# Weight sums and low parts on VectorE, and the keys' second copy by DMA, in an attention kernel with two dense layers

## The chip, the cores and the metric

The kernel runs on one core of one Trainium2 chip. The metric is the time of one execution on the device in microseconds. Three runs of the kernel before took 1054.61, 1055.4 and 1058.65 us; the median is 1055.4 us.

## The reference

Causal attention with a decay per position (4 batches, 8 heads, 576 positions, head size 64), then two dense blocks on 2304 tokens of width 512, each with an inner width of 2048. All in fp32:

```python
scores = q @ k.T / 8 + (cum[:, None] - cum[None, :])     # cum = cumsum(log(clip(f)))
scores = where(causal, -1e9, scores)
x = softmax(scores) @ v                  # heads side by side: 2304 x 512
x = relu(x @ w_in1) ** 2 @ w_out1        # first layer
out = elu(x @ w_in2) @ w_out2            # second layer
```

## The kernel before

Every product is made of three: a number is split into a high part, rounded to the type that TensorE takes (a copy by ScalarE, `AF.Copy`), and a low part, the number minus its high part; then high times high, high times low and low times high are added up (`mm3`, `three`). The low parts are the work of `less` (L131, GpSimd) and `minus` (L115, VectorE or, by `less`, GpSimd). Tables of letters say which engine does which step: a is ScalarE, v VectorE, p GpSimd and, for the keys' copy, d a DMA.

The time falls into these stages:

- **Attention, to about 366 us.** Heads are loaded, scored and applied one after the other. Batch 0 takes plain fp32 operands (`Plain`); batches 1 to 3 take split ones, made by `load_head` (L293) with `part == "F"`, the third letter of each table. Per head: ScalarE copies the raw rows of queries and keys to `qk1` (L312); SP's queue fetches four extra rows into `qk2` (L319); GpSimd subtracts the queries' high part (L320); `kh` copies the keys' high part from `qk1` to `qk2` (L321 to L324, by VectorE); GpSimd subtracts the keys' high part (L325) and splits the values. Scores then take two products, one from `qk1` (L337), one from `qk2` (L338). While heads run, `unit` does half of the first layer for 256 tokens at a time, as filler for TensorE.
- **First layer, the rest, to about 652 us.** `first_layer(j, nxt)` takes blocks j of 512 tokens in the order 3, 4, 0, 1, 2 (block 4 has 256). Blocks 0 to 2 do the inner chunks 8 to 15 here; each chunk has a product `pH`, a `relu2` (relu by ScalarE, square `g` and low part `gl` by VectorE, high part `gh` by ScalarE) and a product into `O`, two chunks later. At a block's end `operands` forms the seven sums that the second layer reads (subtractions on GpSimd, L822; low parts `yl` by GpSimd and VectorE in turn) and stores them by SP's queue (L819).
- **Second layer, from about 652 us.** The inner width is cut into eight pairs of 128-wide chunks, four in the first half, four in the second. `first_product` makes a step's four quarter products from seven products of 128x256 (take and add: `hs`), then elu, `gh` and `gl`; `second_product` follows one step later.

The weights of the second layer come as 64-bit words. `next_w` takes a raw tile, asks SP's queue for the next (`ask_w`, two buffers), and `words` puts the fp32 number together: one ScalarE and four VectorE instructions of 128x512 (L150 to L154). `pair_weights(p)` makes one pair in three steps, each up to a `yield`: first two word tiles, seven high parts of 128x256 by ScalarE (L911), seven low parts (L912) and four sums (L915); then twice one word tile with one high part (L933) and one low part (L934) of 128x512. The chain `wl2` of these steps is advanced at fixed places: three steps beside block 0, four beside block 1 (L1074), five in block 2 (L1077), the rest at the second layer's steps 4 to 6 and 18 to 21 (`w_at`).

Which instruction comes when on each engine is set ahead of the run by a planner (L1150, `schedule_with_timeline_sim=True`): it orders each engine's instructions by their place in the program and by its own cost of each; at run time an engine takes them in that order, and so does SP's queue for DMAs.

Of the kernel before, what the change touches and what calls it, by code (L numbers as in the profile page):

```python
# [43 lines left out]

PLAIN_B = 4
CP = {'pA': 'a', 'pB': 'av', 'xA': 'a', 'xB': 'a'}
ENG = {'qk': 'aaa', 'ql': 'ppp', 'kh': 'pvv', 'kl': 'ppp', 'vh': 'ppp', 'vl': 'ppp', 'xl': 'pv'}
NORM = 'ap'
GL = 'pv'
SQ = 'appp'  # L50
# [19 lines left out]
def f32(ap):  # L70
    return ap.bitcast(F32)
# [10 lines left out]
def attention_then_moe_kernel(ctx, tc, first, firstv, plain, qkv, aug0, f, w1, w2, out):  # L82
    nc = tc.nc
# [31 lines left out]
    def minus(eng, dst, x, hi):  # L115
        if eng == "p":
            less(dst, x, hi)
        else:
            nc.vector.tensor_tensor(dst, x, f32(hi), op=ALU.subtract)  # L119

    def copy(eng, dst, x, scale=None):
        if eng == "a":
            nc.scalar.activation(out=dst, in_=x, func=AF.Copy, scale=1.0 if scale is None else scale)  # L123
        elif eng == "p":
            nc.gpsimd.tensor_scalar(dst, x, 1.0 if scale is None else scale, 0.0, op0=ALU.mult, op1=ALU.add)
        elif scale is None:
            nc.vector.tensor_copy(dst, x)
        else:
            nc.vector.tensor_scalar(dst, x, scale, None, op0=ALU.mult)

    def less(dst, x, hi):  # L131
        nc.gpsimd.tensor_tensor(out=dst, in0=x, in1=f32(hi), op=ALU.subtract)  # L132
# [40 lines left out]
    def win(m, fc, part_, c):  # L173
        return wslot[m, fc][:, part_, c * 128:(c + 1) * 128]

    def wout(m, fc, part_, c=None):
        o = wslot[m, fc][:, part_, 512:1024]
        return o if c is None else o[:, c * 128:(c + 1) * 128]

    def mm3(dst, pairs, first, last, skip=False):  # L180
        n = len(pairs)
        for i, (l, r) in enumerate(pairs):
            nc.tensor.matmul(out=dst, lhsT=l, rhs=r, start=first and i == 0,  # L183
                             stop=last and i == n - 1, skip_group_check=skip)

    def three(hl, hr):
        return [(hl[0], hr[0]), (hl[1], hr[0]), (hl[0], hr[1])]
# [105 lines left out]
    def load_head(b, h, part):  # L293
# [12 lines left out]
        if part == "A":  # L306
            ac = slice(Q0, QW + 256)
            copy(ENG["qk"][w], qk1[:, ac], raw[:, ac])
        else:
            ac = slice(0, RAW)  # L310
            if part == "F":
                copy(ENG["qk"][w], qk1, raw[:, ac])  # L312
            else:
                copy(ENG["qk"][w], qk1[:, qc], raw[:, qc])
                copy(ENG["qk"][w], qk1[:, kc], raw[:, kc])
        if part == "A":
            nc.sync.dma_start(out=f32(qk2[64:68, ac]), in_=f32(ca[g:g + 1]))
        else:
            nc.sync.dma_start(out=f32(qk2[64:68, ac]), in_=aug[g, :, ac])  # L319
        minus(ENG["ql"][w], qk2[0:64, qc], raw[0:64, qc], qk1[0:64, qc])  # L320
        if ENG["kh"][w] == "d":  # L321
            nc.sync.dma_start(out=f32(qk2[0:64, kc]), in_=f32(qk1[0:64, kc]))
# [242 lines left out]
    def relu2(h, n, eng, sq):  # L565
        g = mg.tile([128, 512], F32, tag="g", name="g", bufs=2)
        gh = mg.tile([128, 512], F32R, tag="gh", name="gh")
        gl = mg.tile([128, 512], F32R, tag="gl", name="gl")
        nc.scalar.activation(out=g[:, 0:n], in_=h[:, 0:n], func=AF.Relu)  # L569
        if sq == "a":  # L570
            nc.scalar.activation(out=g[:, 0:n], in_=g[:, 0:n], func=AF.Square)
        else:
            (nc.vector if sq == "v" else nc.gpsimd).tensor_tensor(out=g[:, 0:n], in0=g[:, 0:n], in1=g[:, 0:n], op=ALU.mult)  # L573
        nc.scalar.activation(out=gh[:, 0:n], in_=g[:, 0:n], func=AF.Copy)  # L574
        minus(eng, gl[:, 0:n], g[:, 0:n], gh[:, 0:n])
        return gh, gl
# [63 lines left out]
    def interleave(main, n_main, side, n_side):  # L640
        done = 0
        for i, _ in enumerate(main):
            while done * n_main < (i + 1) * n_side:
                if next(side, "end") == "end":
                    break
                done += 1
        return done

    def chain(gens):
        for g in gens:  # L650
            yield from g
# [129 lines left out]
    def fetch1(j):  # L781
        t0, n = blocks[j]
        xq[j] = []
        for c in range(NC):
            x = x_tile([128, 2, n])
            for off, step, b, s in runs(t0, n):
                nc.sync.dma_start(out=f32(x[:, :, off:off + step]), in_=x1[b][c::NC, :, s:s + step].rearrange("c p t -> p c t"))
            xq[j].append(x)
# [11 lines left out]
    def h_tile():  # L800
        n_ph[0] += 1
        return (ps_H3 if n_ph[0] % 4 else ps_H1).tile([128, 512], F32, tag="H", name="pH")
# [41 lines left out]
    def first_layer(j, nxt):  # L844
        t0, n = blocks[j]
        whole = t0 >= NU * CH
        x = xq.pop(j)
        if nxt is not None:
            fetch1(nxt)
        pr = xa.tile([128, NC, 512], F32, tag="xu", name="pr")  # L850
        if not whole:
            for i in range(n // CH):
                nc.sync.dma_start(out=pr[:, :, i * CH:(i + 1) * CH], in_=part[t0 // CH + i])
        po = [ps_O.tile([128, 512], F32, tag=f"O{c}", name=f"O{c}") for c in range(NC)]
        f0 = 0 if whole else 8

        def second_b(fc, gh, gl):
            for c in range(NC):
                mm3(po[c][:, 0:n], three([wout(1, fc, t, c) for t in range(2)], [gh[:, 0:n], gl[:, 0:n]]), fc == f0, fc == 15)

        pend, depth = [], DEPTH1 * 512 // n
        for fc in range(f0, 16):
            ph = h_tile()
            for c in range(NC):
                mm3(ph[:, 0:n], three([win(1, fc, t, c) for t in range(2)], [x[c][:, 0], x[c][:, 1]]), c == 0, c == NC - 1)
            g = relu2(ph, n, GL[1], "v")
            pend.append((fc, *g))
            if len(pend) > depth:
                second_b(*pend.pop(0))
            yield  # L870
        for p in pend:
            second_b(*p)
        for c in range(NC):
            y = pr[:, c, 0:n]
            if whole:
                nc.vector.tensor_copy(y, po[c][:, 0:n])
            else:
                nc.vector.tensor_tensor(y, po[c][:, 0:n], y, op=ALU.add)
        operands(j, pr)
        yield  # L880
# [13 lines left out]
    def next_w():  # L894
        t = words(ahead.pop(0))
        ask_w()
        return f32(t)

    def w_tile(shape):
        k = n_w[0] % 16  # L900
        n_w[0] += 1
        return (wa, wb)[k // 8].tile(shape, F32R, tag=f"w{k}", name=f"v{k}")

    def pair_weights(p):
        wi = [w_tile([128, 4, 2, 256]), w_tile([128, 3, 2, 256])]
        wo = w_tile([128, 2, 2, 512])
        wp[p] = wi, wo

        def op(a, k):
            h, l = (wi[k // 4][:, k % 4, r] for r in range(2))  # L910
            nc.scalar.activation(out=h, in_=a, func=AF.Copy)  # L911
            less(l, a, h)  # L912

        def add(out, x, y, f):
            nc.gpsimd.tensor_tensor(out=out, in0=x, in1=y, op=f)  # L915

        ta, tb = (next_w() for i in range(2))
        a11, a12, a21, a22 = (t[:, c:c + 256] for t in (ta, tb) for c in (0, 256))
        op(a11, 0)
        op(a12, 5)  # L920
        op(a22, 4)
        add(a22, a21, a22, ALU.add)
        add(a21, a11, a21, ALU.subtract)
        add(a11, a22, a11, ALU.subtract)
        add(a12, a12, a11, ALU.subtract)
        op(a22, 3)
        op(a21, 2)
        op(a11, 1)
        op(a12, 6)
        yield  # L930
        for i in range(2):
            t = next_w()
            nc.scalar.activation(out=wo[:, i, 0], in_=t, func=AF.Copy)  # L933
            less(wo[:, i, 1], t, wo[:, i, 0])  # L934
            yield

    def fetch2(j, ks):
        for k in ks:
            if k >= x2[j].shape[0]:
                continue  # L940
            x = x_tile([128, 2, 2, 256])
            nc.sync.dma_start(out=f32(x).rearrange("p r c t -> p r (c t)"), in_=x2[j][k])
            xq.setdefault(j, []).append(x)
# [126 lines left out]
    ask_w()  # L1070
    ask_w()
    wl2 = chain(pair_weights(p) for p in range(8))
    interleave(first_layer(0, 1), 9, wl2, 3)
    interleave(first_layer(1, 2), 9, wl2, 4)  # L1074
    fetch2(4, range(0, 2))
    for i, _ in enumerate(first_layer(2, None)):
        if i in (3, 4, 5, 6, 7):  # L1077
            next(wl2)
    fetch2(4, range(2, 3))
    fetch2(3, range(0, 6))  # L1080
# [7 lines left out]
    for s, (half, j, p) in enumerate(steps):  # L1088
        q = p % 4
        if q == 0:  # L1090
            x = xq.pop(j)
# [62 lines left out]
```

## Time and profile before

| | |
|---|---|
| median of 3 runs | 1055.4 us |
| profiled execution | 1054.71 us |
| its span, first to last instruction | 1052.7 us |
| busy: TensorE, its weight loads | 1010.2 us (96%), 889.1 us (84%) |
| busy: VectorE, ScalarE, GpSimd | 691.1 us (66%), 545.8 us (52%), 375.4 us (36%) |
| mean granted TensorE clock | 0.997 of full speed |

One execution was taken by the hardware profiler. Times count from the span's start. An engine is busy while one of its instructions runs; for matmuls, which are pipelined, the ends are modelled, so a busy TensorE is not one at its peak. PE is TensorE, PEld its weight loads, DVE VectorE, ACT ScalarE, POOL GpSimd, SP the queue that issues most DMAs. A line is `L` and its number in the kernel; where a helper records the operation (L132 for `less`, L119 for `minus` on VectorE), the tiles tell which step it is: `v` is a tile of the second layer's weights, `wt` a word tile.

### The profile page before, as it was taken

What the parts mean: (1) busy time and instruction counts of PE and PEld (TensorE: products, weight loads), DVE (VectorE), ACT (ScalarE), POOL (GpSimd) and SP (SyncE); (2) the same over time, 40 slices, a digit from 0 to 9 for tenths busy, and PEclk for the clock granted to TensorE, in tenths of its full rate; (3) what the DMA queues carried; (4) which work ended last, traced back from release to release, by engine and by line L of the source; (5) the groups of instructions that cost most, each with busy time, mean ns of one, the idle gap of its engine ahead of it and who ended that gap; (6) DMA issues with size and microseconds to landing.
All of it is one profiled execution on the core that took longest, in us unless ns stands there. A gap on an engine that the chain in (4) does not pass through costs nothing.

```text
span 1052.7 us, 17378 instructions
## 1 busy us (share of the span) xinstructions
PE 1010.2 (96%) x6272; PEld 889.1 (84%) x6272; DVE 691.1 (66%) x1462; ACT 545.8 (52%) x1218; POOL 375.4 (36%) x400
## 2 busy tenths in 40 slices
PE   5899999999999999999999997999999999999998
PEld 3577788999999988889988775898988888899987
DVE  5993587776776548845467858695555878655554
ACT  4865688877886634424343434454334555333331
POOL 3556587576774300012144565440000445000000
PEclk9999999999999999999999999999999999999999
DMA  8843444543431074442645545625315365444502
GB/s 248 240 145 134 153 138 142 181 137 128 160 120 45 33 253 138 122 138 103 201 142 204 193 158 178 225 85 196 132 48 180 124 217 166 134 151 122 169 21 80
DMA packets 71960, 154.91 MB, mean 147 GB/s; under 512 B 8932, under 2 KB 34276, under 8 KB 71844
## 3 DMA queue, kind: packets, MB, share of 16 engines
q1 hardware_dynamic: 71812, 153.75, 44.8%
q8 instruction: 49, 0.80, 0.3%
q14 instruction: 35, 0.29, 0.1%
q10 hardware_dynamic: 64, 0.07, 0.0%
HBM read 115.15 MB, written 39.22 MB: 147 GB/s over the span
## 4 chain that ended last, share of the span: by engine, by line
PE 59%; issue 16%; DVE 12%; POOL 5%; ACT 4%; DMA 3%; SPq 0%; POOLq 0%; ACTq 0%; DVEq 0%
PE O L183 18%; PE pH L183 9%; PE P L183 8%; PE o L183 6%; PE ph L183 6%; PE pt L405 4%; PE pv L412 3%; DVE wt L153 2%; POOL v L132 2%; PE s L337 2%; PE s L338 2%; DVE wt L151 1%; POOL wt L915 1%; DVE wt L152 1%; PE pv L409 1%
## 5 line engine op out<-in xcount | busy, mean ns | idle before, releaser
L183 PEld LDWEIGHTS P<-xu,v 128*128 128x128 f32 x1536 | 200.3, 189 | 12.9 <-ACT hs L995 2.7
L183 PE MATMUL P<-xu,v 128*128 128x256 f32 x1536 | 203.5, 283 | 3.2 <-ACT hs L995 2.5
L183 PE MATMUL O<-v,gh 128*128 128x512 f32 x576 | 172.5, 395 | 0.6 <-ACT gh L966 0.5
L132 POOL TENSOR_TENSOR v<-wt,v 128x256 fp32r<-128x256 f32 (+1 forms) x72 | 72.5, 1015 | 211.7 <-ACT v L911 155.9
L183 PE MATMUL pH<-xu,w 128*128 128x512 f32 (+1 forms) x672 | 140.7, 360 | 0.0
L183 PEld LDWEIGHTS pH<-xu,w 128*128 128x128 f32 x672 | 114.0, 188 | 20.1
L183 PE MATMUL O<-gh,w 128*128 128x512 f32 (+1 forms) x448 | 122.8, 363 | 5.1 <-ACT gh L574 5.1
L183 PEld LDWEIGHTS O<-v,gh 128*128 128x128 f32 x576 | 103.4, 189 | 19.0 <-ACT gh L966 0.7
L995 ACT ACTIVATE hs<-P 128x256 f32<-128x256 f32 x128 | 47.9, 380 | 114.1 <-PE P L183 113.7
L183 PE MATMUL O<-v,gl 128*128 128x512 f32 x288 | 104.2, 394 | 0.5 <-DVE gl L988 0.5
L183 PEld LDWEIGHTS O<-gh,w 128*128 128x128 f32 x448 | 79.7, 189 | 19.9 <-ACT gh L574 6.2
L132 POOL TENSOR_TENSOR qk<-raw,qk 64x704 fp32r<-64x704 f32 (+1 forms) x48 | 78.9, 1643 | 20.4 <-ACT qk L123 15.2
L183 PE MATMUL O<-gl,w 128*128 128x512 f32 (+1 forms) x224 | 80.4, 365 | 3.9 <-DVE gl L119 3.9
L998 DVE TENSOR_TENSOR hs<-P,hs 128x256 f32<-128x256 f32 x96 | 40.4, 421 | 64.3 <-PE P L183 62.6
L132 POOL TENSOR_TENSOR yl<-pr,yh 128x512 fp32r<-128x512 f32 x18 | 24.7, 1371 | 158.7 <-ACT yh L815 108.2
L183 PE MATMUL o<-gh,w 128*128 128x256 f32 x384 | 76.6, 292 | 1.2 <-DVE xB L437 1.2
L150 ACT ACTIVATE wt<-wraw 128x512 f32<-128x512 f32 x57 | 38.2, 671 | 61.6 <-DMA wraw<-in_w_dram 38.6
L574 ACT ACTIVATE gh<-g 128x512 fp32r<-128x512 f32 (+1 forms) x80 | 46.8, 585 | 43.0 <-DVE g L573 39.1
L183 PE MATMUL ph<-xu,w 128*128 128x256 f32 x480 | 67.2, 287 | 1.3 <-DMA xu<-x 1.0
L1024 DVE TENSOR_TENSOR gl<-g,gh 128x512 fp32r<-128x512 f32 x64 | 47.3, 738 | 28.4 <-ACT gh L966 27.9
L573 DVE TENSOR_TENSOR g<-g 128x512 f32<-128x512 f32 (+1 forms) x56 | 45.4, 810 | 28.3 <-ACT g L569 28.2
L183 PEld LDWEIGHTS O<-v,gl 128*128 128x128 f32 x288 | 53.3, 188 | 11.6 <-DVE gl L988 0.8
(151 smaller groups left out, 2122.7 us busy)
## 6 DMA issues: line engine op xcount, KB each, us to landing
xu<-x SPq DMA_DIRECT2D x66, 512.0 KB
wraw<-in_w_dram SPq DMA_DIRECT2D x57, 512.0 KB
raw<-in_qkv_dram SPq DMA_DIRECT2D x24, 800.0 KB
x<-yh SPq DMA_DIRECT2D x31, 256.0 KB
x<-yl SPq DMA_DIRECT2D x31, 256.0 KB
x<-xs SPq DMA_DIRECT2D x16, 320.0 KB
xu<-x SPq DMA_DIRECT2D x16, 256.0 KB
raws_w<-in_w_dram SPq DMA_DIRECT2D x7, 512.0 KB
```

What stands on the lines that cost most here:

```text
L132: nc.gpsimd.tensor_tensor(out=dst, in0=x, in1=f32(hi), op=ALU.subtract)
L150: nc.scalar.activation(out=f32(t), in_=f32(hi), func=AF.Abs)
L153: nc.vector.scalar_tensor_tensor(t, hi, -0x40000000, t, op0=ALU.bitwise_and, op1=ALU.bitwise_or)
L183: nc.tensor.matmul(out=dst, lhsT=l, rhs=r, start=first and i == 0, stop=last and i == n - 1, skip_group_check=skip)
L337: nc.tensor.matmul(out=dst, lhsT=qk1[:, q0:q0 + 128], rhs=qk1[:, QW + j0:QW + j0 + n], start=first, stop=False)
L405: seen[0] = nc.tensor.transpose(dst, src, ident[:, c0:c0 + 128])
L412: seen[0] = nc.tensor.matmul(out=dst, lhsT=hh[2][:, J, :], rhs=hl[i], start=first and i == 0, stop=last and i == 1)
L573: (nc.vector if sq == "v" else nc.gpsimd).tensor_tensor(out=g[:, 0:n], in0=g[:, 0:n], in1=g[:, 0:n], op=ALU.mult)
L574: nc.scalar.activation(out=gh[:, 0:n], in_=g[:, 0:n], func=AF.Copy)
L995: nc.scalar.activation(out=o, in_=x, func=AF.Copy)
L998: nc.vector.tensor_tensor(o, y, x, op=ALU.add)
L1024: nc.vector.tensor_tensor(hl[i][1], gs[i], f32(hl[i][0]), op=ALU.subtract)
```

## The change

It has three parts. The low parts and the sums of `pair_weights` go from GpSimd to VectorE; the subtractions of `operands` (L822) and half of its low parts stay on GpSimd. The third pair's first step moves from the seventh chunk of block 1 to behind the first chunk of block 2; as there are three steps beside block 1 now, pair 1's are spread over the whole block. For the split heads, `kh` becomes a DMA on SP's queue from `qk1` to `qk2`, by a branch that the kernel had (L322).

```diff
-ENG = {'qk': 'aaa', 'ql': 'ppp', 'kh': 'pvv', 'kl': 'ppp', 'vh': 'ppp', 'vl': 'ppp', 'xl': 'pv'}
+ENG = {'qk': 'aaa', 'ql': 'ppp', 'kh': 'pvd', 'kl': 'ppp', 'vh': 'ppp', 'vl': 'ppp', 'xl': 'pv'}
...
         def op(a, k):
             h, l = (wi[k // 4][:, k % 4, r] for r in range(2))
             nc.scalar.activation(out=h, in_=a, func=AF.Copy)
-            less(l, a, h)
+            minus('v', l, a, h)
 
         def add(out, x, y, f):
-            nc.gpsimd.tensor_tensor(out=out, in0=x, in1=y, op=f)
+            nc.vector.tensor_tensor(out, x, y, op=f)
...
             nc.scalar.activation(out=wo[:, i, 0], in_=t, func=AF.Copy)
-            less(wo[:, i, 1], t, wo[:, i, 0])
+            minus('v', wo[:, i, 1], t, wo[:, i, 0])
...
-    interleave(first_layer(1, 2), 9, wl2, 4)
+    interleave(first_layer(1, 2), 9, wl2, 3)
     fetch2(4, range(0, 2))
     for i, _ in enumerate(first_layer(2, None)):
-        if i in (3, 4, 5, 6, 7):
+        if i in (0, 3, 4, 5, 6, 7):
             next(wl2)
```

## Rows read from the trace of the kernel before

**Rows 1.** Busy time by stretch: PE, PEld, DVE, ACT, POOL, granted clock, DMA share, GB/s.
```profile
600.00:675.00 75.00, 65.45 (x320) 53.00 (x319) 54.58 (x75) 32.93 (x63) 46.15 (x42) 1.00 0.57 204
725.00:800.00 75.00, 75.00 (x470) 67.57 (x469) 39.16 (x75) 29.46 (x62) 0.00 (x0) 1.00 0.31 106
815.00:885.00 70.00, 66.22 (x397) 58.43 (x396) 58.98 (x102) 38.76 (x85) 32.83 (x35) 0.98 0.48 160
```

**Rows 2.** The same view, attention with split heads.
```profile
86.00:225.00 139.00, 135.03 (x971) 119.24 (x970) 91.93 (x286) 105.47 (x262) 96.96 (x105) 1.00 0.43 140
```

**Rows 3.** Waits of PE, 600 to 680 us: total, times, longest.
```profile
PE O L183 <- ACT gh L574: 5.1, 3, 2.4
PE O L183 <- DVE gl L119: 3.9, 5, 1.6
```

**Rows 4.** Timeline at 600 us: start, duration, engine, line; idle before in brackets.
```profile
599.53 0.66 ACT L150 ACTIVATE wt<-wraw 128x512 f32<-128x512 f32 x1 [2.73 <-DMA wraw<-in_w_dram]
...
602.12 0.50 PE L183 MATMUL O<-gh,w 128*128 128x512 f32 x1 [1.36 <-ACT gh L574]
```

**Rows 5.** Timeline at 638 us.
```profile
638.05 1.28 POOL L132 TENSOR_TENSOR v<-wt,v 128x512 fp32r<-128x512 f32 x1 [2.24 <-ACT v L933]
638.05 1.56 DVE L152 TENSOR_SCALAR wt<-wt 128x512 int32<-128x512 int32 x1
```

**Rows 6.** Groups of DVE, 725 to 800 us: busy us, mean ns | idle before.
```profile
L1024 DVE TENSOR_TENSOR gl<-g,gh 128x512 fp32r<-128x512 f32 x14 | 9.7, 692 | 7.0 <-ACT gh L966 6.8
...
L1017 DVE TENSOR_SCALAR g<-hs 128x512 f32<-128x512 f32 x7 | 3.0, 427 | 0.2
L1016 DVE TENSOR_TENSOR hs<-hs 128x256 f32<-128x256 f32 x7 | 3.0, 425 | 3.1 <-ACT hs L995 3.0
```

**Rows 7.** Timeline at 648 us.
```profile
647.67 0.42 ACT L911 ACTIVATE v<-wt 128x256 fp32r<-128x256 f32 x1 [1.49 <-POOL wt L915]
```

**Rows 8.** Instructions with a word tile, by stretch: DVE, ACT, POOL busy (count).
```profile
600.00:675.00 75.00, 21.54 (x28) 12.13 (x25) 23.29 (x26) 1.00 0.57 204
815.00:885.00 70.00, 24.84 (x40) 17.27 (x35) 32.83 (x35) 0.98 0.48 160
```

**Rows 9.** Groups of DVE, 600 to 675 us.
```profile
L119 DVE TENSOR_TENSOR gl<-g,gh 128x512 fp32r<-128x512 f32 x9 | 8.6, 953 | 5.4 <-ACT gh L574 5.4
...
L153 DVE SCALAR_TENSOR_TENSOR wt<-wraw,wt 128x512 int32<-128x512 int32 x7 | 6.8, 968 | 0.2
L152 DVE TENSOR_SCALAR wt<-wt 128x512 int32<-128x512 int32 x7 | 6.6, 940 | 0.2
L119 DVE TENSOR_TENSOR yl<-pr,yh 128x512 fp32r<-128x512 f32 x6 | 6.5, 1089 | 4.0 <-DMA x<-yl 2.2 <-ACT yh L815 1.2 <-POOL v L132 0.6
```

**Rows 10.** Groups of DVE, 815 to 885 us.
```profile
L1024 DVE TENSOR_TENSOR gl<-g,gh 128x512 fp32r<-128x512 f32 x12 | 10.0, 831 | 4.7 <-ACT gh L966 4.5
...
L1016 DVE TENSOR_TENSOR hs<-hs 128x256 f32<-128x256 f32 x6 | 4.0, 668 | 0.0
L1017 DVE TENSOR_SCALAR g<-hs 128x512 f32<-128x512 f32 x6 | 4.0, 663 | 0.1
```

**Rows 11.** The tile `qk`: ns min/median/max; below, who waited for it (us, times).
```profile
L127 DVE CAST qk<-qk x24: 442/480/1923, 87.4 to 318.1; 64x576 fp32r<-64x576 f32 x24
...
  DVE qk L127: 12.1, 13
```

**Rows 12.** Timeline of one head at 300 us: cast, two subtractions, first score.
```profile
300.70 0.45 DVE L127 CAST qk<-qk 64x576 fp32r<-64x576 f32 x1 [1.10 <-ACT qk L123]
...
301.45 3.24 POOL L132 TENSOR_TENSOR qk<-raw,qk 64x704 fp32r<-64x704 f32 x2
...
305.83 0.36 PE L337 MATMUL s<-qk 128*128 128x256 f32 x1
```

**Rows 13.** The chain that ended last, a landing at 132 us.
```profile
131.89 4.87 DMA xu<-x
```

**Rows 14.** Waits of SP's queue: total, times, longest.
```profile
SPq L448 <- DVE xs L119: 60.6, 13, 10.4
```

## The prediction

> **What bounds the kernel now.** I read the busy time by stretch first. TensorE is the busiest engine and mostly has no gap: in 725 to 800 us it is busy for 75.00 of 75 us [rows 1]. What can be won is the time in which it waits. After the start-up there are three places with such time: 86 to 225 us (attention, 139 − 135.03 = 4.0 us idle [rows 2]), 600 to 675 us (end of the first layer, 75 − 65.45 = 9.55 us) and 815 to 885 us (70 − 66.22 = 3.8 us; the granted clock there is 0.98 in the mean, so some 0.04 of the stretch ran at 1.2 instead of 2.4 GHz, which cost about 1.4 us more) [rows 1]. Together that is 18.7 us, 1.8% of the span. Then I read the waits: who ended TensorE's. In 600 to 680 us they are ScalarE's `gh` and VectorE's `gl` [rows 3]. GpSimd, from which the change takes work, ends none of the two. So it counts only by what it holds up on the other two.
>
> In order of time around these waits, the trace shows three ways. At 599.5 us ScalarE, which takes its instructions in order, sat idle for 2.73 us before the third pair's second word group, because its raw weights had not landed; the relu behind it came late and TensorE waited 1.36 us for `gh` [rows 4]. At 638.05 us a GpSimd subtraction of 1.28 us and a VectorE shift start together, and the shift takes 1.56 us where a one-input instruction of that size takes 0.427 us without GpSimd [rows 5, 6]. At 647.7 us ScalarE sat 1.49 us until a GpSimd sum was done, with the next `gh` queued behind [rows 7].
>
> **The change, part by part.**
>
> *Lows and sums go to VectorE, stretch 600 to 675 us.* GpSimd does 26 of these instructions there in 23.29 us [rows 8]: 4 of 128x512 (two for each of two pairs), the other 22 of 128x256. On VectorE, a two-input 128x256 subtraction or sum takes 0.425 us (L1016) and a 128x512 one 0.692 us (L1024) [rows 6]. So VectorE gains 22 × 0.425 + 4 × 0.692 = 12.1 us of work. It loses a part of what it now spends beside GpSimd: `gl` 9 × (0.953 − 0.692) = 2.3 us, L152 7 × (0.940 − 0.427) = 3.6 us, `yl` 6 × (1.089 − 0.692) = 2.4 us, L153 7 × (0.968 − 0.692) = 1.9 us, 10.2 us in all [rows 6, 9]. Of GpSimd's 46.15 us there [rows 1], 23.29 go away; the subtractions of L822 and the `yl` stay. So about half, 5.1 us, is relief (bounds: none and 10.2). VectorE goes from 54.58 to 61.6 of 75 us: fuller, not full. Of TensorE's 9.55 us I count these as gone: the wait at 602 us and its echo, 1.9 us, since the third pair's words now come after the layer's end; some 2 us of waits behind ScalarE's stops for GpSimd sums; half of the other 5.6 us, which follow stretched VectorE instructions. Against that, 12.1 us of new work ahead of some squares and `gl` may delay TensorE; I put 1.7 us. Result: −5 us (bounds −9.5, when all waits go, and +3.5, when half of the net new 7.0 us of VectorE work lands on TensorE).
>
> The Trainium skill, SBUF — State Buffer, section Who interferes with whom, says that a VectorE instruction with two SBUF inputs contends with a GpSimd instruction that reads SBUF, and that the one that issues second waits until the first is done. The trace agrees (1.56 us against 0.427 [rows 5, 6]). It speaks against the change: the moved instructions have two SBUF inputs themselves, so they would stand still behind L822 and the `yl` as others do now. If this ate the relief, VectorE would have 66.7 of 75 us here and I would put this part at 0, the sum at 1055 us: the first rival below.
>
> *The third pair's step is later.* Its two word groups, seven copies, seven lows, four sums and two fetches of raw weights on SP's queue move from the last chunks of block 1 to behind the first chunk of block 2, past block 1's fourteen operand stores and the two operand fetches of L1075. Pair 1's steps spread over the same block. Between the new place and the first product that reads the third pair lie seven chunks of block 2 and the products of the first two pairs, most of the 75 us; so I cost the delay at nothing. If that cover were gone, TensorE would wait for weights, which it does nowhere now: its waits there are for `gh` and `gl` [rows 3]. The gain of 1.9 us above is this edit's.
>
> *Lows and sums in 815 to 885 us.* Here pairs 5 to 7 are made beside the second layer, and GpSimd does nothing else: 35 instructions, 32.83 us [rows 1, 8], 4 large (pairs 5 and 6) and 31 small. On VectorE: 31 × 0.425 + 4 × 0.692 = 15.9 us. Relief: `gl` 12 × (0.831 − 0.692) = 1.7, L1016 6 × (0.668 − 0.425) = 1.5, L1017 6 × (0.663 − 0.427) = 1.4, together 4.6 us [rows 6, 10]; the 40 word instructions took 24.84 us [rows 8] where 20 × 0.692 + 20 × 0.427 would be 22.4, another 2.4 us. So +15.9 − 7.0 = +8.9 us, and VectorE goes from 58.98 to 67.9 of 70 us, 97%. This is the weak place. For it: the chain of a pair's seven copies and four sums gets shorter, as a step of some 0.9 us on GpSimd (32.83 us for 35) becomes 0.425, and the lock that stretched instructions is gone entirely. Against it: no room is left. Bounds: −5.2 us (all of the 3.8 + 1.4 goes) and +9 us (all net work lands on TensorE). I take +1, nearer the middle.
>
> *The keys' second copy by DMA.* VectorE loses 24 casts (median 0.480 us, the longest 1.923) and the 12.1 us in 13 places in which it stood for ScalarE's copy [rows 11]. New on SP: 24 DMAs of 64 × 576 × 4 bytes = 147 KB, each of which stands until ScalarE's copy is done, up to 1.27 us, with the stores of x1, the fetches of x1 and of later heads queued behind. Cover: the head at 299 us has its cast at 300.70 us, GpSimd's two subtractions of the same head end at 304.69 and its first score is at 305.83 [rows 12]. A landing has taken up to 4.87 us in the chain [rows 13], so from 0 to 5.1 us after the cast's start, that is still no wait. No row shows this DMA itself, so its landing is bounded by that. TensorE's idle time in attention is 4.0 us [rows 2]; VectorE has 92 of 139 us busy there, and its waits are only some of the causes. I take −1 us (bounds −4 and +4, the latter by the third rival). After 225 us TensorE has no gap to speak of until 600 us, so what is won early stays won.
>
> Sum: −5 + 1 − 1 = −5 us. The profiled execution took 1054.71 us (span 1052.7, 2.0 us around it), 0.7 us under the median of 1055.4. 1054.7 − 5 = 1049.7, so **1050 us**. A planner fixes each engine's order ahead of the run and will choose other orders from 86 us on; no row tells which, and I allow 2 us either way for it.
>
> **Rivals.**
> 1. *No change*: the waits of 600 to 675 us move from `gh` behind GpSimd to `gl` behind longer VectorE queues, and the early gain is lost in 815 to 885 us. For it: `gl` already ends 3.9 us of waits [rows 3]. GpSimd keeps 46.15 − 23.29 = 22.9 us in 600 to 675 us, behind which the moved instructions can stand still as L152 does now. Against: ScalarE's stops [rows 4, 7] have causes that go. Time: 1054 to 1055 us.
> 2. *VectorE becomes the bound* (slower). Place: 815 to 885 us, then 600 to 675. Each low now stands in VectorE's queue for ScalarE's copy of its quarter, with `hs`, `g` and `gl` of the running products behind it. If the lows wait there, or GpSimd's lock stays, it pays +9 us in the later stretch and +3.5 in the earlier, with nothing won but the 1 us in attention: 1054.7 + 11.5 = 1066 us; where only half of it comes true, 1060. It decides from the point where VectorE can't hold 90% busy in 815 to 885 us: 67.9 / 0.9 = 75 us of work time in a 70 us stretch. For it: VectorE is already busy 58.98 of 70 us. Against: 11 us of idle time there are mostly ScalarE and GpSimd steps that get shorter.
> 3. *SP holds the copy*: the new DMA stands in order behind a store that waits for its x; such waits at L448 took up to 10.4 us [rows 14]. Scores would start late while TensorE has little other work, before 225 us: about 4 us lost in place of 1 won, 1055 us with the rest.
>
> **How the numbers follow.** Forecast 45% (own range 1046 to 1053), rival 1 25%, rival 2 20%, rival 3 10%. A larger gain, all of the 9.5 us and some of the rest, reaches 1043 us; rival 2 at half price 1060 and more. Range 1043 to 1062 us. What a measurement of this kernel can tell from no change is about 0.5%, 5.3 us: faster is under 1050.1, slower over 1060.7 us. The forecast stands on the border, so I give two thirds of it and the larger gains to faster: 0.47; same 0.33; slower 0.20.
>
> **What would show it.** Right: TensorE's idle time in the 75 us before the second layer falls to 4 or 5 us, no stop of ScalarE on raw weights just before the end of block 1, word instructions near 0.43 and 0.69 us while pairs 5 to 7 are made, GpSimd empty there, VectorE at 90% or more. Wrong: TensorE waits for weights or `hs` of pairs 6 and 7 for more than 5 us, the granted clock falls there for longer; scores that wait for the DMA of the keys; `gl` waits of over 9 us before the second layer.

## The result, and the profile after

| | before | after |
|---|---|---|
| median (4 runs each) | 1056.63 us | 1040.42 us |
| ratio, 95% interval | | 0.9854 [0.9812, 0.9897] |
| profiled execution, its span | 1054.71, 1052.7 us | 1038.76, 1036.7 us |

The kernel became 1.5% faster, about 16 us. The direction was the forecast's; the size was three times its 5 us, and the time lies below the range of 1043 to 1062 us.

Where in the run the 16 us lie is told by one row of each profile: the products of the first layer's first half, of which the last ends the attention stage. The fields after the count are the shortest, median and longest duration in ns, and the start of the first and the last one. Before:

```profile
L183 PE MATMUL ph<-xu,w x480: 276/283/387, 126.5 to 365.9; 128*128 128x256 f32 x160
```

After:

```profile
L183 PE MATMUL ph<-xu,w x480: 276/283/388, 126.8 to 366.0; 128*128 128x256 f32 x160
```

The last one starts at the same time, so all is won behind it: from 366 us to the end of the span it was 1052.7 − 365.9 = 686.8 us and is 1036.7 − 366.0 = 670.7 us. I call this the tail below.

The busy time of the whole span after (engine, us, share, instructions):

```profile
PE 1007.4 (97%) x6272; PEld 889.6 (86%) x6272; DVE 679.6 (66%) x1542; ACT 546.7 (53%) x1218; POOL 272.8 (26%) x296
```

VectorE took over 104 instructions from GpSimd, gave 24 casts away, and is busy for 679.6 us where it was for 691.1. TensorE's idle time went from 1052.7 − 1010.2 = 42.5 to 29.3 us, and its busy time fell by 2.8 us. By stretch (length, then busy time of PE, PEld, DVE, ACT, POOL, granted clock, DMA share, GB/s); the stretches are set some 11 us earlier than those of [rows 1], as the work is:

```profile
86.00:225.00 139.00, 135.18 (x970) 119.16 (x970) 81.40 (x270) 104.98 (x262) 94.75 (x107) 1.00 0.52 162
600.00:661.00 61.00, 61.00 (x314) 51.90 (x313) 54.23 (x97) 30.09 (x56) 14.59 (x10) 1.00 0.52 185
661.00:675.00 14.00, 13.49 (x82) 11.82 (x80) 9.10 (x16) 5.79 (x13) 7.39 (x6) 1.00 0.70 250
804.00:870.00 66.00, 66.00 (x401) 58.66 (x401) 60.70 (x136) 38.02 (x83) 0.00 (x0) 1.00 0.48 163
870.00:890.00 20.00, 19.33 (x132) 17.66 (x131) 16.74 (x37) 11.48 (x25) 0.00 (x0) 1.00 0.56 203
```

Read the second and fourth row against [rows 1]: TensorE has no gap left where it had 9.55 and 3.78 us, though VectorE is busy for 54.23 of 61 us and for 60.70 of 66 us, 89% and 92%. The whole list of TensorE's waits from 366 us to the end (total, times, longest):

```profile
PE O L183 <- ACT gh L966: 1.6, 1, 1.6
PE P L183 <- DMA xu<-x: 0.7, 2, 0.4
```

The waits of [rows 3] for `gh` and `gl` are gone. In 680 to 700 us VectorE is even busy for the whole stretch, and TensorE has no gap:

```profile
680.00:700.00 20.00, 20.00 (x134) 18.34 (x134) 20.00 (x47) 12.12 (x28) 0.00 (x0) 1.00 0.42 133
```

VectorE's groups in 804 to 870 us (busy us, mean ns | idle before) show why the extra work found room:

```profile
L1024 DVE TENSOR_TENSOR gl<-g,gh 128x512 fp32r<-128x512 f32 x13 | 8.9, 685 | 0.1
L119 DVE TENSOR_TENSOR v<-wt,v 128x256 fp32r<-128x256 f32 x18 | 7.5, 419 | 0.5 <-ACT v L911 0.5
L152 DVE TENSOR_SCALAR wt<-wt 128x512 int32<-128x512 int32 x10 | 4.2, 422 | 0.0
L915 DVE TENSOR_TENSOR wt<-wt 128x256 f32<-128x256 f32 x10 | 4.2, 421 | 0.1
L1017 DVE TENSOR_SCALAR g<-hs 128x512 f32<-128x512 f32 x6 | 2.5, 421 | 0.0
L1016 DVE TENSOR_TENSOR hs<-hs 128x256 f32<-128x256 f32 x6 | 2.5, 419 | 0.0
```

`gl` takes 685 ns where it took 831, L1016 419 for 668, L1017 421 for 663 [rows 10]: the durations of [rows 6], without GpSimd. In 600 to 661 us GpSimd still has L822 and half of the `yl`, and VectorE's instructions beside them are stretched as before:

```profile
L573 DVE TENSOR_TENSOR g<-g 128x512 f32<-128x512 f32 x8 | 8.6, 1076 | 0.7 <-ACT g L569 0.6
L119 DVE TENSOR_TENSOR gl<-g,gh 128x512 fp32r<-128x512 f32 x8 | 6.9, 866 | 0.8 <-ACT gh L574 0.7
L119 DVE TENSOR_TENSOR v<-wt,v 128x256 fp32r<-128x256 f32 x14 | 5.8, 419 | 0.5 <-ACT v L911 0.5
L119 DVE TENSOR_TENSOR v<-wt,v 128x512 fp32r<-128x512 f32 x4 | 3.8, 958 | 0.0
```

The square of a chunk (L573) takes 1076 ns, and of the moved lows the four large ones take 958 ns for 688 elsewhere; the fourteen small ones, though, take their undisturbed 419.

### The profile page after: what moved, and what is told of

The parts are those of the page before. It is cut to its first block, busy times and chain, and to the rows that moved or that the text cites. A ratio compares the mean times of both kernels' runs of the same rounds, so it can differ in the third digit from the quotient of the medians.

```text
span 1036.7 us, 17366 instructions
## 1 busy us (share of the span) xinstructions
PE 1007.4 (97%) x6272; PEld 889.6 (86%) x6272; DVE 679.6 (66%) x1542; ACT 546.7 (53%) x1218; POOL 272.8 (26%) x296
## 4 chain that ended last, share of the span: by engine, by line
PE 82%; DVE 7%; DMA 5%; ACT 3%; POOL 1%; issue 1%; SPq 0%; ACTq 0%; POOLq 0%; DVEq 0%
PE O L183 29%; PE P L183 16%; PE pH L183 11%; PE o L183 6%; PE ph L183 6%; PE pt L405 4%; PE pv L412 4%; PE s L338 2%; PE s L337 2%; PE s L333 1%; DMA x<-yl 1%; DVE wt L153 1%; DMA xu<-x 1%; DMA wraw<-in_w_dram 1%; PE pv L409 1%
## 5 line engine op out<-in xcount | busy, mean ns | idle before, releaser
L183 PE MATMUL O<-v,gh 128*128 128x512 f32 x576 | 169.4, 394 | 1.6 <-ACT gh L966 1.6
L183 PE MATMUL O<-v,gl 128*128 128x512 f32 x288 | 100.9, 393 | 0.0
L132 POOL TENSOR_TENSOR qk<-raw,qk 64x704 fp32r<-64x704 f32 (+1 forms) x48 | 75.7, 1577 | 21.6 <-ACT qk L123 16.3
L1020 ACT ACTIVATE g<-g 128x512 f32<-128x512 f32 x64 | 40.2, 629 | 54.3 <-DVE g L1012 32.4
L966 ACT ACTIVATE gh<-g 128x512 fp32r<-128x512 f32 x72 | 45.4, 631 | 36.3 <-DVE g L1021 29.4
L573 DVE TENSOR_TENSOR g<-g 128x512 f32<-128x512 f32 (+1 forms) x56 | 45.4, 812 | 27.8 <-ACT g L569 27.7
L183 PEld LDWEIGHTS ph<-xu,w 128*128 128x128 f32 x480 | 60.8, 190 | 1.8 <-DMA xu<-x 1.3
```

Source lines behind the costliest of these rows:

```text
L966: nc.scalar.activation(out=gh, in_=g, func=AF.Copy)
L1020: nc.scalar.activation(out=gs[i], in_=gs[i], func=AF.Exp)
```

## The experiments

The times of different groups of runs are not set side by side; each kernel has its ratio to the kernel before in the same group. The tail is read from each kernel's one profile, as above. It leaves out the first 366 us, because the profiled executions differ there by chance: the kernel after has its last `ph` product at 366.0 us in one execution and at 372.8 us in another, with tails of 670.7 and 670.0 us. "Idle" is TensorE's, in 600 to 700 and in 804 to 900 us.

| kernel | median, us | ratio [95%] | tail, us | idle, us |
|---|---|---|---|---|
| before | | 1 | 686.8 | 9.55, 3.78 |
| after | 1040.42 | 0.9854 [0.9812, 0.9897] | 670.7 | 1.61, 0.67 |
| after, a second time | 1040.93 | 0.9846 [0.9807, 0.9884] | 670.0 | 1.82, 0.14 |
| e1: lows and sums alone | 1041.53 | 0.9843 [0.9817, 0.9869] | 669.4 | 0.03, 0.20 |
| e2: the DMA alone | 1052.53 | 0.9965 [0.9944, 0.9987] | 683.2 | 8.70, 3.55 |
| e3: the later step alone | 1056.24 | 0.9992 [0.9974, 1.001] | 685.5 | 6.57, 4.11 |
| e4: after, without the DMA | 1041.63 | 0.9851 [0.9824, 0.9878] | 670.0 | 1.18, 0.11 |
| e5: after, sums on GpSimd | 1046.09 | 0.9887 [0.9836, 0.9938] | 675.3 | 2.59, 1.55 |
| e6: after, lows on GpSimd | 1050.39 | 0.9904 [0.987, 0.9938] | 678.1 | 4.64, 2.38 |
| e7: after, idle reads for the lows | 1049.37 | 0.9908 [0.9875, 0.9941] | 679.4 | 4.61, 1.53 |
| e8: after, more VectorE work | 1048.6 | 0.992 [0.9892, 0.9949] | 679.4 | 4.18, 4.10 |
| e9: after, without the later step | 1036.88 | 0.9819 [0.9782, 0.9856] | 668.3 | 0.42, 0.12 |
| e10: after, idle reads for the sums | 1042.82 | 0.9874 [0.9821, 0.9926] | 674.4 | 3.50, 1.11 |
| e11: after, idle writes | 1042.3 | 0.9859 [0.9817, 0.9901] | 671.7 | 1.93, 0.20 |

The theory (in the expectations, the lock): GpSimd's instructions stretch VectorE's beside them, and TensorE waited for what came late by that. The rival: the lows and sums themselves were late on GpSimd, since its steps take longer, and what waited for them was late in turn (the chain). Two more theories were that the DMA or the later step brings the gain. A last rival holds for every run: the planner orders each kernel's instructions anew, so a time can change by the order alone. Read off the traces behind 373 us, without the instructions that write `spare`, ScalarE's and VectorE's instructions stand in e4 and e10 in exactly the order of after, and in e11 but for one exchange of two on ScalarE; in e7, 86 of ScalarE's 562 places and 108 of VectorE's 844 differ.

**e1, the lows and sums alone**, on the kernel before:

```diff
-            less(l, a, h)
+            minus('v', l, a, h)
...
-            nc.gpsimd.tensor_tensor(out=out, in0=x, in1=y, op=f)
+            nc.vector.tensor_tensor(out, x, y, op=f)
...
-            less(wo[:, i, 1], t, wo[:, i, 0])
+            minus('v', wo[:, i, 1], t, wo[:, i, 0])
```

> Only the low parts and sums go to VectorE; the third pair's step stays in block 1 and the cast on VectorE. Theory (GpSimd beside VectorE made the waits of both late stretches): 12 to 15 us faster than before, 1042 to 1045 us, TensorE idle under 4 us from 600 us to the second layer and under 2 us while pairs 5 to 7 are made. Rival (the later step removed the waits at the end of the first layer): at most 6 us faster, TensorE still idle for 5 us or more at the end of block 1 and in block 2.

The whole gain is this part's: TensorE's idle time meets the theory, and the time is a little better than its 12 to 15 us. In the very stretches of [rows 1], e1 has:

```profile
600.00:675.00 75.00, 74.97 (x393) 64.02 (x392) 60.39 (x104) 36.14 (x68) 23.50 (x16) 1.00 0.59 207
815.00:885.00 70.00, 69.80 (x437) 62.43 (x436) 64.06 (x143) 41.06 (x90) 0.00 (x0) 1.00 0.56 196
```

TensorE is busy for 74.97 of 75 and 69.80 of 70 us, at full clock. VectorE does 41 instructions more in the second stretch and is busy for 64.06 us, 5.1 more than before, not the 8.9 of the prediction; as the work stands some 11 us earlier in e1, a stretch that holds all of it in both is the fairer one: in 804 to 900 us it is 84.12 us for 77.89, 6.2 more. Over the whole span:

```profile
PE 1007.3 (97%) x6272; PEld 889.8 (86%) x6272; DVE 696.5 (67%) x1566; ACT 546.8 (53%) x1218; POOL 277.5 (27%) x296
```

VectorE took 104 instructions that are some 48 us of work at the durations above (56 × 0.419 + 16 × 0.688 + 32 × 0.421, an estimate), and its busy time rose by 5.4 us, from 691.1 to 696.5.

**e2, the DMA alone**, on the kernel before:

```diff
-ENG = {... 'kh': 'pvv', ...}
+ENG = {... 'kh': 'pvd', ...}
```

> Only the keys' second copy becomes a DMA. Theory: within 0.2% of before (attention's idle time of TensorE is 3.97 us before and 3.82 us after). Rival (freed VectorE time in attention is worth time): 2 to 4 us faster, TensorE idle from 86 to 225 us under 2.5 us.

It is worth 0.35% (0.13 to 0.56%), 3.6 us of tail. The theory's 0.2% lies within that; the rival's time came, but not its idle time: in 86 to 225 us TensorE's is 3.96 us, before 3.97. One place can be named, behind attention: before, TensorE stood for 1.22 us in 366 to 375 us, for VectorE's `xB`:

```profile
366.00:375.00 9.00, 7.78 (x66) 7.68 (x65) 1.48 (x3) 1.93 (x4) 2.33 (x2) 1.00 0.63 177
```

With the DMA alone:

```profile
366.00:375.00 9.00, 9.00 (x77) 9.00 (x77) 1.48 (x3) 2.14 (x4) 2.34 (x2) 1.00 0.62 194
```

The planner's order is another there. Profiles with the DMA (after, e2, e9) have no gap in this stretch, those without it (before, e1, e3, e4) have 1.22 us. Idle time in 600 to 700 and 804 to 900 us is 0.85 and 0.23 us less, and the granted clock in 804 to 900 us is 1.00 for 0.98; I put those down to the order that the planner chose; no run separates it from the copy.

**e3, the later step alone**, on the kernel before:

```diff
-    interleave(first_layer(1, 2), 9, wl2, 4)
+    interleave(first_layer(1, 2), 9, wl2, 3)
...
-        if i in (3, 4, 5, 6, 7):
+        if i in (0, 3, 4, 5, 6, 7):
```

> Only the third pair's first step moves; lows and sums stay on GpSimd. Theory: 0 to 3 us faster, the wait at the end of block 1 goes, those of block 2 stay or grow as two pairs now fall into it. Rival: 6 us or more faster.

Alone it is worth nothing that can be measured, as the theory allowed. The waits of 600 us go, and others come:

```profile
600.00:675.00 75.00, 70.74 (x341) 58.24 (x339) 58.66 (x77) 32.26 (x60) 43.65 (x40) 0.98 0.55 193
```

TensorE is idle for 4.26 us here instead of 9.55, but the clock is 0.98 and TensorE's busy time over the whole run is 1014.0 us, 3.8 more than before.

**e4, after with VectorE's cast back** (`'pvd'` to `'pvv'`):

> The changed kernel with the keys' cast back on VectorE. Theory: as the changed kernel, 1040 us within 0.2%, 24 casts back at a median of 0.48 us. Rival: 2 to 4 us slower than the changed kernel.

The same as after, in time and tail: beside the lows and sums the DMA adds nothing that can be measured.

**e5, after with the sums on GpSimd, and e6, after with the lows on GpSimd**:

```diff
-            nc.vector.tensor_tensor(out, x, y, op=f)
+            nc.gpsimd.tensor_tensor(out=out, in0=x, in1=y, op=f)
```

```diff
-            minus('v', l, a, h)
+            less(l, a, h)
...
-            minus('v', wo[:, i, 1], t, wo[:, i, 0])
+            less(wo[:, i, 1], t, wo[:, i, 0])
```

> The changed kernel with the four sums of each pair back on GpSimd, low parts on VectorE. Lock theory (a GpSimd instruction beside VectorE stretches VectorE's, in proportion to GpSimd's busy time): about a third of the gain is lost, 1045 to 1047 us. Chain theory (ScalarE and VectorE stand in order behind slow sums, as the low parts and copies wait for them): most of it is lost, 1048 us or more, with ScalarE stopped behind L915.

> The changed kernel with the low parts back on GpSimd, sums on VectorE. Lock theory: about two thirds of the gain are lost, 1048 to 1052 us. Chain theory (nothing on the way to TensorE waits for a low part except the sums that overwrite a word tile): little is lost, 1040 to 1044 us.

By the tails, the 32 sums give back 4.9 us (675.3 − 670.4, the mean of the two executions of after) and the 72 lows 7.7 us of the 16.4. Both count. The medians, 1046.09 and 1050.39 us, lie in the ranges of the lock theory and outside those of the chain, but the ratios' intervals are 1.0 and 0.7% wide and the planner's order differs from that of after, so I don't take these two runs to tell the lock from the chain.

**e7, after with idle reads for the lows.** Each low stays on VectorE; for each 128x256 of it, GpSimd subtracts the high part from itself into a tile `spare` that nobody reads (twice for a 128x512 low):

```diff
             minus('v', l, a, h)
+            nc.gpsimd.tensor_tensor(out=spare, in0=f32(h), in1=f32(h), op=ALU.subtract)
```

> The changed kernel, and for each low part GpSimd also subtracts the high part from itself, into a tile that nobody reads; the output is the reference's. GpSimd is then about as busy beside VectorE as before for the low parts, and no instruction of another engine waits for it but the next use of the weight tile. Lock theory: 6 us or more of the gain are lost, VectorE's word and elu instructions are stretched again in mean, 1046 to 1054 us. Chain theory: 1040 to 1042 us.

Work that nobody waits for gives back 9.0 us of the 16.4 of tail, as much as the lows themselves do in e6 (7.7), and in the trace no instruction of another engine waits for a `spare`. So for the lows the chain falls. How much of the 9.0 us is the planner's other order is open; e10 has no such doubt. The intervals of the ratios overlap a little (this one starts at 0.9875, those of after end at 0.9897 and 0.9884), so the finding rests on the tails and on the durations. The stretch 804 to 890 us of e7:

```profile
804.00:890.00 86.00, 84.61 (x517) 74.82 (x516) 81.05 (x161) 46.94 (x103) 27.36 (x29) 1.00 0.49 159
```

and VectorE's groups in it:

```profile
L119 DVE TENSOR_TENSOR v<-wt,v 128x256 fp32r<-128x256 f32 x21 | 11.2, 536 | 0.5 <-ACT v L912 0.5
L917 DVE TENSOR_TENSOR wt<-wt 128x256 f32<-128x256 f32 x12 | 7.1, 589 | 0.1
L152 DVE TENSOR_SCALAR wt<-wt 128x512 int32<-128x512 int32 x12 | 6.1, 512 | 0.1
L1016 DVE TENSOR_SCALAR g<-hs 128x512 f32<-128x512 f32 x7 | 4.2, 596 | 0.0
```

The lows take 536 ns for 419, the sums 589 for 421, the shift 512 for 422, the elu's first minimum (L1016 here, L1012 in the kernel after) 596 for 420. VectorE is at 94% with fewer instructions done.

**e8, after with more VectorE work**: after each 128x256 low one more subtraction into `spare`, on VectorE:

```diff
             minus('v', l, a, h)
+            nc.vector.tensor_tensor(spare, f32(h), f32(h), op=ALU.subtract)
```

> The changed kernel, and for each of the seven low parts of 128x256 VectorE does one more subtraction of that size into a tile that nobody reads. It adds 7 x 0.42 = 2.9 us per pair, some 7.6 us where pairs 5 to 7 are made, where VectorE is busy 60.70 of 66 us in the changed kernel. If VectorE's free time were the limit there (the prediction's second rival): 3 to 8 us slower than the changed kernel, TensorE idle there. If the weights' chain still has slack behind the running products: within 2 us of the changed kernel.

21 such instructions of 415 ns, 8.7 us, fall into 804 to 890 us, and the tail is 9.0 us longer, a little more than the expectation's upper case. The same stretch, that of 600 to 700 us, and TensorE's two costliest waits in 600 to 900 us:

```profile
804.00:890.00 86.00, 81.90 (x515) 73.47 (x514) 79.79 (x185) 46.86 (x102) 0.00 (x0) 1.00 0.52 172
...
600.00:700.00 100.00, 95.82 (x515) 82.70 (x514) 87.58 (x163) 47.23 (x93) 23.66 (x16) 0.97 0.48 168
```

```profile
PE O L183 <- ACT gh L968: 3.6, 2, 2.9
PE P L183 <- ACT v L912: 3.1, 1, 3.1
```

So more work on VectorE can cost time, and in 804 to 890 us TensorE waits for weights too (`v`). But no share of busy time is the limit: VectorE is at 93% here with 4.1 us of TensorE's idle time, in e7 at 94% with 1.39, and in the kernel after at 100% for 20 us with none. And more than half of the 9.0 us arises in 600 to 700 us, where VectorE is busy for 87.58 us, as in after (86.87): TensorE is idle for 2.4 to 2.6 us more there, one wait for `gh` takes 2.9 us, and behind it the clock is below full speed, which at 0.97 over 100 us is some 3 us. The planner's order is another too. Whether the sum of the work, its place between a low and the next copies, or the order does it, this run doesn't tell.

**e9, after without the later step** (the diff of e3 undone):

> The changed kernel with the third pair's first step back in block 1: lows and sums on VectorE and the DMA, without the move. If the move cured the stop of ScalarE at the end of block 1 (the prediction's 1.9 us): 1.5 to 2 us slower than the changed kernel. If the stop came from GpSimd's slow sums, which kept the word tiles and so the fetches of raw weights back: no slower, 1038 to 1040 us, as the profile of the kernel with lows and sums alone has no wait there.

The lowest ratio of all, and 2.1 us of tail less than after; the intervals of the two ratios overlap, so whether it beats the kernel after is open. Its 600 to 700 us and TensorE's waits from 366 us to the end:

```profile
600.00:700.00 100.00, 99.58 (x552) 86.46 (x551) 83.94 (x157) 51.12 (x100) 23.50 (x16) 1.00 0.52 180
```

```profile
PE O L183 <- ACT gh L574: 0.4, 1, 0.4
```

TensorE's wait at the end of block 1, to which the prediction gave 1.9 us for the later step, is gone without that step. A stop of ScalarE on raw weights is still there, one word group earlier and 2.61 us long (in e1 2.55, before 2.73), but TensorE doesn't wait behind it:

```profile
590.57 0.66 ACT L150 ACTIVATE wt<-wraw 128x512 f32<-128x512 f32 x1 [2.61 <-DMA wraw<-in_w_dram]
```

So the time came as expected and the reason given with it, GpSimd's slow sums holding back the fetches, isn't shown. And the kernels with the later step (after, both times, and e4) have a wait that e9 and e1 don't have, in after at 676 us:

```profile
672.29 1.28 POOL L822 TENSOR_TENSOR pr<-pr 128x512 f32<-128x512 f32 x1 [0.63 <-DVE yl L119]
672.58 1.28 DVE L1012 TENSOR_SCALAR g<-hs 128x512 f32<-128x512 f32 x1
...
676.10 1.19 PE L183 MATMUL O<-v,gh 128*128 128x512 f32 x4 [1.61 <-ACT gh L966]
```

The elu's first minimum (L1012), 0.42 us when undisturbed, takes 1.28 us beside a GpSimd subtraction; its `gh` is late by that and by what ScalarE does between.

**e10, after with idle reads for the sums**: after each sum on VectorE, GpSimd subtracts it from itself.

```diff
             nc.vector.tensor_tensor(out, x, y, op=f)
+            nc.gpsimd.tensor_tensor(out=spare, in0=out, in1=out, op=ALU.subtract)
```

> The changed kernel, and after each of the four sums of a pair GpSimd subtracts the sum from itself into a tile that nobody reads; the output is the reference's. Lock theory: 2 to 6 us slower than the changed kernel, about as with the sums themselves on GpSimd (1046 us). Chain theory for the sums (their order and slowness held the copies back): within 1.5 us of the changed kernel.

4.0 us of tail given back, where the sums themselves gave back 4.9. The medians alone wouldn't tell this (1042.82 us, after 1040.93 beside it, with overlapping intervals); the tail and the trace do. ScalarE and VectorE do the same instructions in the same order as in after, and the sums, which take 420 ns there, take 657:

```profile
L916 DVE TENSOR_TENSOR wt<-wt 128x256 f32<-128x256 f32 x12 | 7.9, 657 | 0.1
```

TensorE waits for `gh` three times, 3.4 us, in after once, 1.6 us. One of the new waits can be followed instruction by instruction. From the same L154 (644.68 us in e10, 643.49 in after) to the same `gh` (656.30 and 653.89) both kernels do the same, and e10 takes 1.2 us longer; one sum takes 0.83 us and three lows 0.73, 0.80 and 0.52 where after has 0.42 each, 1.2 us in all, and none of them waits for GpSimd. TensorE then waits for that `gh`, as it doesn't in after:

```profile
647.87 0.83 DVE L916 TENSOR_TENSOR wt<-wt 128x256 f32<-128x256 f32 x1
...
656.98 1.19 PE L183 MATMUL O<-v,gh 128*128 128x512 f32 x4 [1.15 <-ACT gh L968]
```

In the whole run one instruction waits for a `spare`, 0.8 us on ScalarE. So the stretching alone can make TensorE wait, with neither a chain behind GpSimd nor another order on these two engines, and most of what the sums cost is stretching as well; a share of the chain of up to 1 us stays open, as the intervals of e5 and e10 overlap.

**e11, after with idle writes.** As e7, but GpSimd reads only 4 columns of the high part (so that it keeps its place behind ScalarE's copy) and then fills `spare` twice:

```diff
             minus('v', l, a, h)
+            nc.gpsimd.tensor_scalar(spare[:, 0:4], f32(h[:, 0:4]), 1.0, 0.0, op0=ALU.mult, op1=ALU.add)
+            nc.gpsimd.memset(spare, 0.0)
+            nc.gpsimd.memset(spare, 0.0)
```

> As with the idle subtractions for the low parts, but GpSimd only writes: a four-element copy that holds it until the high part is there, then two fills of 128x256 (four for the large ones). GpSimd is about as long busy. If its reading of SBUF stretches two-input VectorE instructions, and its writing only one-input ones: 1 to 4 us slower than the changed kernel, gl and sums not stretched, L151, L152 stretched. If any busy GpSimd does it: 8 us slower, as before.

Nothing is given back beyond 1.3 us of tail, and the clock can account for that: it is 0.98 in 600 to 700 us, where after has 1.00. GpSimd's groups in 804 to 890 us:

```profile
L906 POOL TENSOR_SCALAR spare<-v 128x4 f32<-128x4 f32 x33 | 14.0, 424 | 135.8 <-ACT v L917 114.5 <-ACT v L940 19.3 <-POOL spare L908 0.4
L907 POOL MEMSET spare<- 128x256 f32 x33 | 11.5, 347 | 2.0
L908 POOL MEMSET spare<- 128x256 f32 x33 | 11.3, 341 | 1.9
```

It is busy for 36.7 us there, against 27.36 in e7, and most of VectorE's groups take what they take without it:

```profile
L119 DVE TENSOR_TENSOR v<-wt,v 128x256 fp32r<-128x256 f32 x21 | 8.7, 415 | 0.5 <-ACT v L917 0.5
L152 DVE TENSOR_SCALAR wt<-wt 128x512 int32<-128x512 int32 x12 | 5.3, 438 | 0.0
L922 DVE TENSOR_TENSOR wt<-wt 128x256 f32<-128x256 f32 x12 | 5.0, 420 | 0.1
L1021 DVE TENSOR_SCALAR g<-hs 128x512 f32<-128x512 f32 x9 | 4.1, 458 | 0.0
```

So it is not that GpSimd is busy or takes its turn behind the copies; for VectorE's lows and sums it is that its instructions read. The Trainium skill, SBUF — State Buffer, section Who interferes with whom, says that a VectorE instruction with two SBUF inputs contends with a GpSimd instruction that reads SBUF and not with one that only writes; for the lows and sums the two runs agree (536 and 589 ns beside reads, 415 and 420 beside fills). The same section of the Trainium skill says that some instructions with one input, tensor_scalar among them, can contend with GpSimd without that limit to reads, when they run in a mode that takes both ports (no run here shows the mode itself); by that e11's expectation had L151 and L152 stretched. The means show little of it (L152 438 ns beside fills, 512 beside reads, 422 without GpSimd; L1021, the elu's first minimum, 458 for 420), but single instructions do:

```profile
836.23 0.47 POOL L907 MEMSET spare<- 128x256 f32 x1
836.37 0.61 DVE L152 TENSOR_SCALAR wt<-wt 128x512 int32<-128x512 int32 x1
```

The shift starts 0.14 us after a fill, takes 0.61 us where it takes 0.42 undisturbed, and ends 0.28 us after the fill does. Three more of e11's one-input instructions beside a fill take 0.55 us or more (at 537.95, 823.49 and 866.77 us), each ending 0.28 us after the fill; of the lows and sums in 804 to 890 us, none takes more than 0.43 us for a 128x256 one or 0.70 for a 128x512 one. So fills do hold up one-input instructions; at about 0.34 us a fill it costs little. How much of e7's cost is reading and how much is that its subtractions are longer (0.86 and 1.16 us) isn't separated for these.

**After, a second time**, with e9 to e11:

> The changed kernel once more, beside the others on the same chip: 0.985 of before, 1040 to 1042 us.

The same ratio and tail as the first time.

## Why the prediction was wrong in size

- **What bounds the kernel**: right. TensorE's waits in the two stretches were what could be won, and they went. Its sentence that GpSimd "counts only by what it holds up on the other two" was the right mechanism; that it ends no wait of TensorE hid its size. e10 and e7 put the price on it: with reads that nobody waits for, waits come back, and 4.0 and 9.0 us of tail with them. Every sign that the prediction named for being right came (no such stop of ScalarE, word instructions at 0.42 and 0.69 us, GpSimd empty while pairs 5 to 7 are made, VectorE over 90%), with less idle time left than it said.
- **Lows and sums, 600 to 675 us, −5 us**: mis-sized. The idle time went from 9.55 to 1.61 us in 600 to 700 us, 7.9 us, near the term's better bound. The reckoning took half of the relief and half of the waits, and left out the squares (L573, 858 ns there, where a two-input instruction of that size takes 692 undisturbed [rows 6]); e1, with this edit alone, shows all of the waits gone. The charge of 1.7 us for new work ahead of `gl` was not there: no `gl` ends a wait any more.
- **Lows and sums, 815 to 885 us, +1 us**: the step that failed. It summed +8.9 us of net VectorE work, called 97% busy "no room", and took a value between the bounds. Measured, it is the better bound: 3.1 us of waits gone and the clock at 1.00 for 0.98, which the prediction put at 1.4 us. The relief was too small in the sum, too. Two of VectorE's groups in 815 to 885 us of the kernel before were not counted:

```profile
L1021 DVE SCALAR_TENSOR_TENSOR g<-g,hs 128x512 f32<-128x512 f32 x12 | 9.3, 772 | 2.0 <-ACT g L1020 2.0
...
L1012 DVE TENSOR_SCALAR g<-hs 128x512 f32<-128x512 f32 x6 | 3.6, 603 | 0.0
```

  Against 686 and 420 ns in the kernel after they are 12 × 0.086 + 6 × 0.183 = 2.1 us, and the word instructions' excess, 10 times each of L151 to L154, is 3.3 us by group means instead of 2.4. That makes 10 us of relief instead of 7.0, and some 6 us of net work, as e1 has (5.1 or 6.2 by the stretch). But even a right net sum would have been charged for nothing: what TensorE had waited for was stretched instructions ahead of `gh` and `gl`, not a full VectorE, and 92% busy was not a bound. That more work can become a cost is shown by e8, at what point is not.
- **The later step, 1.9 us within the first term**: wrong. It is worth nothing alone (e3), TensorE's wait goes without it, though ScalarE still stops on raw weights, one word group earlier (e1, e9), and beside the rest it brings the 1.61 us wait at 676 us. The cover that the prediction named for the third pair's weights held: no wait for `v`.
- **The keys' copy, −1 us**: the place was wrong, and that the size looks right is luck. Attention's idle time is 3.82 us for 3.97 [rows 2]; 1.2 us are won at 367 us, by the planner's order. Alone the copy brings 3.6 us of tail (e2), beside the lows and sums nothing that can be measured (e4). The rival of SP's queue didn't come. One head after (compare [rows 12]):

```profile
298.58 1.26 ACT L123 ACTIVATE qk<-raw 128x1280 fp32r<-128x1280 f32 x1
299.86 0.47 SPq L322 DMA_DIRECT2D qk<-qk  x1
...
306.56 0.36 PE L337 MATMUL s<-qk 128*128 128x256 f32 x1
```

  The DMA is issued 0.02 us after the copy; the scores start 6.7 us later. SP's queue stood in front of it for 15.2 us in ten places, 3.3 us at most:

```profile
SPq L322 <- ACT qk L123: 15.2, 10, 3.3
```

  and of its 24 landings TensorE waited for one, 0.6 us.
- **Rival 1**, the lock that stays behind L822 and `yl`: true in part. L573 takes 1076 ns and the four large lows 958, as it said, the fourteen small lows and the sums their undisturbed 419 and 421, and TensorE doesn't wait for them in 600 to 661 us. The row that the prediction put beside the two-input rule, 1.56 us for 0.427 [rows 5, 6], is of an instruction with one input; the row that bears on that rule is `gl`, 953 ns for 692 [rows 6, 9]. **Rival 2**, VectorE as the bound: it was given 90% as its point; after stands at 92% without a wait, and e8 and e7 show that the share of busy time doesn't set the point. The 11 us of idle time that the prediction held against it were ended by ScalarE and TensorE, none by GpSimd.
- **The sum**: 7.9 + 3.1 + 1.4 + 1.2 = 13.6 of 16.0 us. The other 2.4 us are busy time of TensorE that is no longer spent; the records don't tell on what. In e1 the same gain comes without the 1.2 us, so the split is that of this pair of profiles.

## What to carry to other kernels

An engine that ends none of the bounding engine's waits can still be what costs the time: compare each group's mean duration near it with the same group where it is idle, and take the whole difference as its price, for every group and not for the worst few. Where one engine stretches another's instructions, moving its work to the other can add far less busy time than the work itself (here 5.4 us for some 48); the other's busy share alone says little until it begins to end waits. To tell lateness from disturbance, let the engine do the same work on data that nobody waits for, and see from the traces that the order of the other engines' instructions stayed the same. A mean over a group hides single instructions that ran beside the disturber: look at those too.

## What was not expected of the hardware

GpSimd busy for 36.7 of 86 us with fills and 4-column copies left VectorE's durations within 4% in its lows, sums and shifts (415, 420 and 438 ns for 419, 421 and 422) and within 9% in the elu's first minimum (458 for 420), though single one-input instructions took 0.55 to 0.61 us; 27.36 us of reading subtractions lengthened the lows, sums and shifts by 21 to 40% (536, 589 and 512 ns). VectorE ran at 92% busy for 66 us, and at 100% for 20 us, without one wait of TensorE.
